# S4D convolution beside a sigmoid GLU on one core: GpSimd's share of the spectral products ahead of the weights, the first column half's last stage by quarters, another order of the frequency steps

## The chip, the cores and the metric

The kernel runs on one core of a Trainium2 chip. The metric is device time in microseconds (us) from the first to the last instruction of one launch. The engines carry the names that the profile gives them: PE (TensorE) with its weight loads PEld, DVE (VectorE), ACT (ScalarE), POOL (GpSimd), SP (SyncE, which here only issues DMAs).

## The reference, cut to what matters

```python
# L = 2048 tokens, D = 448 channels, N = 256 states, F = 1792
x  = A_u
xn = layernorm(x)
# part A: diagonal state space model as a long convolution
dt = exp(log_dt); A = -exp(log_A_real) + 1j * A_imag; C = (C_real + 1j * C_imag) * dt
K  = 2 * einsum("dn,dnl->dl", C, exp(A * dt * pos)).real          # one kernel of 2048 taps per channel
y  = irfft(rfft(xn, 4096) * rfft(K, 4096), 4096)[:2048] + xn * D_skip
# part B: GLU
h  = sigmoid(xn @ w_gate) * (xn @ w_up)
out = x + y + h @ w_down
```

## The kernel before, in words

Two generators, `conv()` and `glu()`, write the program. A loop at the bottom of the kernel calls whichever of them has the smaller `done[i] / total[i]`; each `yield` says how much work, in the planner's own units, was just written. `total` (L1141) holds the two sums. For `conv()` the last term is `17 * WS`, one `WS` for each frequency step of the last stage. So these two numbers decide how far the GLU has come when the convolution reaches a given point. Afterwards a list scheduler orders the instructions of each engine by its own estimate of times; `hp(HP)` around an instruction raises its priority there by 300. What an engine's queue then holds is run strictly in that order.

The GLU goes through fourteen tiles of 128 rows of F for the first 1024 tokens (half 0) and again for the second 1024 (half 1). For each tile and each block of 512 tokens, `gate` (L692) writes two groups of 11 matmuls (`gu`, L710): the gate half and the up half, each in three parts, because every float is split into a high and a low part (`wh`/`wl` for weights, `xh`/`xl` for tokens). ACT takes tanh of the gate group (`th`), DVE multiplies (`hf`, L721), ACT and DVE split the product (`hh` L726, `hl` L728). After a group of two or three tiles come the down matmuls (`po`, L824; 9 matmuls for each 128 tokens of a group of three) with DVE's addition into `acc` (L829). In half 1 five weight tiles are loaded and split by GpSimd itself: DMA of `wraw` from GpSimd's queue (L645, L647), `wh` (L772), `wl` (L773), DMA of `rdw` (L653), `dh` (L798), `dl` (L799). `wraw` and `rdw` share one buffer, so for one tile these steps follow each other. The others come back split from memory through SP's queue.

The convolution has three stages: constants; a generation stage `kgen` that builds the kernel's first transform (products `ko`, L619, from `Et` and `Ft` of DVE, L603 to L605); and `spectra`, the last stage. This has 17 steps of two kinds of columns: for each of two column halves h (224 channels each), eight groups of four frequencies named by k, in the order `ks`, and once k = 32 for both. One step is:

- `there` (L908): 32 small matmuls each into two PSUM tiles `pk` (the kernel's spectrum) and `px` (the input's). ACT copies one half of each (`oo`, L912); DVE forms sum and difference (`kk`, `xx`, L914 and L915). When these are done, `pk` and `px` are free again.
- the products: `yy` (L919) and `kk` (L920) on DVE, then two instructions on GpSimd, the differences of the one (L921) and the sums of the other (L922), then `sd` (L924, L925) on DVE. There is one buffer of `yy` and of `kk`.
- `back` (L937) of the step before, into the same `pk` and `px`; ACT copies them to `vt` (L943) and SP writes that to memory (`v_d`): one DMA for each half of the partitions (L957), but for k = 0 three (L953, L955).

When all eight groups of a column half are written, `vp` is read back (L963) and `last` (L973) makes the outputs of that half from it, in four quarters of four token blocks q = 0 to 3: 32 matmuls into `pk` for an even q, into `px` for an odd one, followed by DVE's additions (L982). For h = 0 the quarters come two at a time, behind two consecutive steps; for h = 1 all four come at the very end, between the GLU's last down matmuls. `out` hands the finished rows of the h = 0 half to SP, ACT and GpSimd in turn for writing.

On PE the program fixes the order of the two streams by hand: `sp_mm` and `glu_mm` hold the last matmul of the one and of the other, and every group is told to issue behind it.

Of the kernel before, what the change touches and what calls it, by code (L numbers as in the profile page):

```python
# [15 lines left out]
ALU = mybir.AluOpType  # L16
# [12 lines left out]
NFT = F // 128  # L29
WK = 5.5  # L30
WS = 7.0
HOLE = 6
AHEAD = 46
WP = 5
WX = 2
HELD = 9
LATE = 3.6
HP = 300
Y0 = (8, 1)
# [13 lines left out]
NCK = D // DC  # L53
# [74 lines left out]
def s4d_glu_kernel(ctx, tc, io):  # L128
    nc = tc.nc
    hp = tc.high_priority  # L130
# [107 lines left out]
    def out_end(src, b0, ds, engs=(nc.sync, nc.scalar)):  # L238
        for g in range(4):
            to = blocks(out_t, g, b0, src.shape[1])  # L240
            engs[g % len(engs)].dma_start(to[:, :, ds], src[32 * g : 32 * g + 32, :, ds])
# [606 lines left out]
    def spectra(pf):  # L848
# [16 lines left out]
        def work(n, sh, bufs):  # L865
            return spare[n].pop() if spare.get(n) else pf.tile(sh, F32, name=n, bufs=bufs)
# [22 lines left out]
        def after():  # L889
            return tc.issue_after(sp_mm[0].ins)  # L890

        def there(k, tb, sk, sx):

            n = 2 if k == 32 else 4
            np_ = 32 * n
            both = []
            for j, src in enumerate((sk, sx)):
                with after():
                    for c in range(2):
                        for g in range(n):  # L900
                            for p in range(2):
                                s = slice(64 * p, 64 * p + 64)
                                to = pb[j][32 * g : 32 * g + 32, p, H * c : H * c + H]
                                rhs = sx[s, g]
                                if src is sk:
                                    to, rhs = to.rearrange("p (g d) -> p g d", d=32), sk[s, :, g]
                                w = (t32[s, 0] if k == 32 else tb[s, g])[:, 32 * c : 32 * c + 32]
                                mm = nc.tensor.matmul(to, w, rhs, start=True, stop=True, skip_group_check=True)  # L908
                sp_mm[:] = [mm]
                ev, od = (half(pb[j][:np_, p, : 2 * H]) for p in range(2))  # L910
                oo = work("oo", [128, 2, H], 2)
                nc.scalar.copy(oo[:np_], od)  # L912
                t = work(("kk", "xx")[j], [128, 2, 2, H], 1)
                v.tensor_tensor(t[:np_, 0], ev, oo[:np_], ALU.add)  # L914
                v.tensor_tensor(t[:np_, 1], ev, oo[:np_], ALU.subtract)  # L915
                both.append(t[:np_])
            kk, xx = both
            yy = work("yy", [128, 2, 2, H], 1)[:np_]
            v.tensor_tensor(yy, kk, xx, ALU.mult)  # L919
            v.tensor_tensor(kk, kk, xx[:, :, ::-1], ALU.mult)  # L920
            nc.gpsimd.tensor_tensor(yy[:, :, 0], yy[:, :, 0], yy[:, :, 1], ALU.subtract)  # L921
            nc.gpsimd.tensor_tensor(yy[:, :, 1], kk[:, :, 0], kk[:, :, 1], ALU.add)  # L922
            sd = work("sd", [128, 2, 2, H], 2)
            v.tensor_tensor(sd[:np_, 0], yy[:, 0], yy[:, 1], ALU.add)  # L924
            v.tensor_tensor(sd[:np_, 1], yy[:, 0], yy[:, 1], ALU.subtract)  # L925
            return sd
# [32 lines left out]
        def turned(h, k, n=8):  # L959
            if h not in vp:  # L960
                vp[h] = pf.tile([128, 32, H], F32, name="vp", bufs=1)
            s = slice(k // 4, 128, n)
            nc.sync.dma_start(vp[h][s], v_d[h, s])  # L963

        def last(h, q):

            for p in range(2):
                s = slice(64 * p, 64 * p + 64)
                for i in range(2):
                    for g in range(4):  # L970
                        w = 16 * (q % 2) + 4 * g + 2 * (q // 2) + i
                        with after():
                            mm = nc.tensor.matmul(  # L973
                                pb[q % 2][32 * g : 32 * g + 32, p, H * i : H * i + H], wf[s, w], vp[h][s, w],
                                start=True, stop=True, skip_group_check=True,
                            )
            sp_mm[:] = [mm]
            ds = slice(H * h, H * h + H)
            acc = ac[:, 4 * q : 4 * q + 4] if q < 2 else accs[q]
            for p in range(2):  # L980
                a = acc[:, p::2, ds]
                v.tensor_tensor(a, a, half(pb[q % 2][:, p, : 2 * H]), ALU.add)  # L982
            if h == 1 and q < 3:
                out_end(acc, 4 * q, ds, *([[nc.gpsimd]] if q == 0 else []))
            elif h == 0 and q < 2:
                out(acc, 4 * q, h)
# [2 lines left out]
        lasts.append(last)  # L989
        nc.sync.dma_start(t32, io["c_t32"])  # L990
        nc.gpsimd.dma_start(bk, io["c_bk"])
        ks = [4, 20, 0, 16, 8, 24, 12, 28]
        steps = [(0, k) for k in ks] + [(1, k) for k in ks[-NTB:] + ks[:-NTB]]
        steps[1:1] = [(None, 32)]
        tabs = {}
        ld = [loads(*s) for s in steps[:NLD]]
        nc.gpsimd.dma_start(wf, io["c_wf"])
        prev, wait, due = None, [], []
        for n, (h, k) in enumerate(steps):

            sp_mm[:] = glu_mm
            cur = there(k, *ld[n])
            if (h, k) == (0, ks[-NTB - 1]):
                for k_ in ks[:-NTB]:
                    tabs.pop(k_)
            if n + NLD < len(steps):
                ld.append(loads(*steps[n + NLD]))
            glu_on[:] = [1]
            yield WS / 2
            sp_mm[:] = glu_mm  # L1010
            if prev is not None:
                back(*prev)
            if 4 <= n < 8:
                o = slice(2 * n - 8, 2 * n - 6)
                nc.sync.dma_start(ac[:, o], acc_d[:, o])
            if prev is not None and prev[1] < 32:
                wait.append(prev[:2])

            while len(wait) > 2 and not (due and wait[0][0] == 1):
                t, u = wait.pop(0), wait.pop(0)  # L1020
                turned(*t, 4)
                if u == (0, 28):
                    due = [n + 1]
            prev = (h, k, cur)
            if n == 11:
                total[1] -= LATE
            yield WS / 2
            if due and n >= due[0]:
                sp_mm[:] = glu_mm
                for q in (0, 1, 2, 3)[2 * (n - due[0]) : 2 * (n - due[0]) + 2]:  # L1030
                    last(0, q)
                if n == due[0] + 1:
                    due = []
        sp_mm[:] = glu_mm
# [95 lines left out]
    lasts, glu_mm, sp_mm, glu_on, outs, x1s, hfs, xls = [], [], [], [], [0], [0], [], []  # L1130
    xq, psc, raws, acl, marks, slots, pqs = list(x_first), [], [], [], [None, None], {}, []
    W1s, GGs, act = [], [], []
    gens = [conv(), glu()]
    total = [sum(Y0) + 11 * WP + 8 * WX + AHEAD + NCK * WK + HOLE + 17 * WS, 2 * (4 + NFT * 14.8) - HELD]
    done = [0.0, 0.0]
    done[0] += next(gens[0])
    held = False
# [38 lines left out]
```

## Time and profile before

| | us |
|---|---|
| three runs | 757.61, 762.92, 768.84 |
| median | 762.92 |
| the profiled execution's own time | 769.57 |
| its span, first to last instruction | 767.8 |
| busy: PE, DVE, POOL, ACT | 678.1, 602.3, 427.1, 423.1 |
| mean granted TensorE clock | 0.945 |

In a row of the timeline stand the start, the duration, the engine, the line, the operation, the output and the input, the number of instructions, and in brackets the idle time of the engine before it with what ended it. In the chain of waits stand start, duration and what ran. A row of the waits has the total, the number and the longest one. In a row of the windows come the stretch, its length, then the busy time of PE, PEld, DVE, ACT and POOL, the granted clock, the DMA engines' share and GB/s.

### The profile page before, as it was taken

Reading aid. Unit: us, or ns where it says so; the run is one execution under the profiler, and the core shown is the slowest. Engines: PE = TensorE matmul, PEld = TensorE weight load, DVE = VectorE, ACT = ScalarE, POOL = GpSimd, SP = SyncE. Lnnn points to the kernel's source line nnn. Section 1 sums busy time; section 2 is a strip of 40 time slices with the busy share of each in tenths; the row PEclk is TensorE's granted clock in tenths of the full one; section 3 lists DMA queues with packets and bytes.
Section 4 is the critical chain, followed back from the end, with each engine's and each line's share of the span. In section 5 each row is a group of like instructions: output and inputs, shape, how many; then the busy total and the mean of one; then the engine's idle time right before and its main releaser. Section 6 shows DMA issues by size and latency. Waiting matters only on the chain.

```text
span 767.8 us, 22542 instructions
## 1 busy us (share of the span) xinstructions
PE 678.1 (88%) x9477; PEld 520.6 (68%) x9477; DVE 602.3 (78%) x777; ACT 423.1 (55%) x651; POOL 427.1 (56%) x455
## 2 busy tenths in 40 slices
PE   3897699999998988888899999899899799968966
PEld 2664588877876877555778777788667567645754
DVE  6798996789998998876659988787397567777843
ACT  3544466477787888787377777767413222212310
POOL 2110065748889889974636776754146553675211
PEclk9997989999999999798999999999999999988997
DMA  9934265345234543344744134304588757775464
GB/s 209 208 126 160 79 200 178 117 137 177 78 102 151 180 118 96 116 151 144 229 136 146 38 95 141 93 20 142 149 260 233 213 159 205 214 206 163 114 161 126
DMA packets 93462, 114.58 MB, mean 149 GB/s; under 512 B 12848, under 2 KB 83056, under 8 KB 93104
## 3 DMA queue, kind: packets, MB, share of 16 engines
q1 hardware_dynamic: 71632, 92.54, 41.1%
q10 hardware_dynamic: 19248, 14.91, 6.9%
q0 software_dynamic: 2480, 5.67, 2.8%
q8 instruction: 75, 1.23, 0.7%
q14 instruction: 27, 0.22, 0.1%
HBM read 68.32 MB, written 44.76 MB: 147 GB/s over the span
## 4 chain that ended last, share of the span: by engine, by line
PE 34%; DVE 9%; issue 4%; POOL 4%; DMA 4%; ACT 2%; SPq 1%; ACTq 0%; DVEq 0%; POOLq 0%
PE gu L710 14%; PE po L824 7%; PE ko L619 4%; PE tr L535 2%; POOL yy L921 1%; DMA v_d<-vt 1%; POOL yy L922 1%; PE pk L908 1%; DVE yy L919 1%; DVE Ft L605 1%; DVE sd L925 1%; PE kp L561 1%; PE px L908 1%; DMA wraw<-in_B_w_up_dram 1%; DMA rdw<-in_B_w_down_dram 1%
## 5 line engine op out<-in xcount | busy, mean ns | idle before, releaser
L513 POOL TENSOR_TENSOR me<-me,pm 128x32 f32<-128x32 f32 (+1 forms) x168 | 147.5, 878 | 84.3 <-DVE Et L604 69.6
L513 POOL TENSOR_TENSOR mf<-mf,pm 128x64 f32<-128x64 f32 (+1 forms) x112 | 122.7, 1095 | 6.1
L710 PE MATMUL gu<-xh,wh 128*128 128x512 f32 x336 | 107.8, 431 | 6.4 <-DVE acc L829 4.8
L710 PE MATMUL gu<-xh,wl 128*128 128x512 f32 x336 | 99.5, 404 | 0.0
L710 PE MATMUL gu<-xl,wh 128*128 128x512 f32 x336 | 98.3, 397 | 0.5 <-DVE xl L218 0.5
L824 PE MATMUL po<-dh,hh 128*128 128x448 f32 (+1 forms) x227 | 87.1, 384 | 10.0 <-DVE hf L721 3.8
L605 DVE TENSOR_TENSOR Ft<-mf,S 128x1024 f32<-128x1024 f32 x56 | 80.5, 1437 | 13.5 <-PE ko L619 4.4
L604 DVE TENSOR_TENSOR Et<-me,S 128x1024 f32<-128x1024 f32 x56 | 79.1, 1412 | 14.2 <-ACT me L526 14.2
L710 PEld LDWEIGHTS gu<-xh,wh 128*128 128x128 f32 x336 | 64.6, 203 | 30.2 <-issue 10.0
L824 PE MATMUL po<-dl,hh 128*128 128x448 f32 (+1 forms) x227 | 84.1, 370 | 0.0
L603 DVE TENSOR_TENSOR Et<-me,S 128x1024 f32<-128x1024 f32 x56 | 77.3, 1384 | 8.2 <-ACT S L546 7.9
L824 PE MATMUL po<-dh,hl 128*128 128x448 f32 (+1 forms) x227 | 82.8, 368 | 0.0
L543 ACT ACTIVATE S<-tr 128x1024 f32<-128x1024 f32 x56 | 57.7, 1031 | 43.6 <-PE tr L535 28.8
L726 ACT CAST hh<-hf 128x512 fp32r<-128x512 f32 x56 | 34.9, 623 | 78.3 <-DVE hf L721 77.7
L619 PEld LDWEIGHTS ko<-Et,Ft 128*32 128x32 f32 x3584 | 56.1, 115 | 30.3 <-DVE Ft L605 13.6
L710 PEld LDWEIGHTS gu<-xh,wl 128*128 128x128 f32 x336 | 66.0, 197 | 15.1
L619 PE MATMUL ko<-Et,Ft 128*32 128x64 f32 x3584 | 65.9, 228 | 11.5 <-DVE Ft L605 11.5
L710 PEld LDWEIGHTS gu<-xl,wh 128*128 128x128 f32 x336 | 63.7, 191 | 16.0 <-issue 1.4
L546 ACT ACTIVATE S<-S,hpi 128x1024 f32<-128x1024 f32 x56 | 65.6, 1171 | 0.0
L721 DVE SCALAR_TENSOR_TENSOR hf<-th,gu 128x512 f32<-128x512 f32 x56 | 38.1, 680 | 32.8 <-PE gu L710 26.1
L829 DVE SCALAR_TENSOR_TENSOR acc<-po,acc 128x448 f32<-128x448 f32 (+1 forms) x81 | 48.2, 608 | 18.6 <-PE po L824 18.6
L728 DVE TENSOR_TENSOR hl<-hf,hh 128x512 fp32r<-128x512 f32 x56 | 51.4, 918 | 14.3 <-ACT hh L726 14.2
(212 smaller groups left out, 1357.9 us busy)
## 6 DMA issues: line engine op xcount, KB each, us to landing
sk_d<-sk ACTq DMA_DIRECT2D x14, 512.0 KB
sx<-x_d SPq DMA_DIRECT2D x64, 112.0 KB
skl<-sk_d SPq DMA_DIRECT2D x16, 448.0 KB
vp<-v_d SPq DMA_DIRECT2D x7, 896.0 KB
v_d<-vt SPq DMA_DIRECT2D x27, 224.0 KB
wt_d<-wh SPq DMA_DIRECT2D x9, 512.0 KB
wt_d<-wl SPq DMA_DIRECT2D x9, 512.0 KB
wl<-wt_d SPq DMA_DIRECT2D x9, 512.0 KB
```

What stands on the lines that cost most here:

```text
L513: ins = nc.gpsimd.tensor_tensor(m[:, :, w + a : 2 * w : n], m[:, :, a:w:n], par(base + i).unsqueeze(2).to_broadcast([128, 4 * DC, w // n]) ...
L543: nc.scalar.activation(rows(cs), pv, AF.Abs)
L546: sins[:] = [nc.scalar.activation(cs, cs, AF.Sin, scale=-TWO_PI, bias=hpi)]
L603: v.tensor_tensor(Et[:, :, :, 32:64], two(me[:, :, 32:64]), S[:, 1::-1], ALU.mult)
L604: v.tensor_tensor(Et[:, :, :, 0:32], two(me[:, :, 0:32]), S[:, 1:3, :, ::-1], ALU.mult)
L605: fts[:] = [v.tensor_tensor(Ft, two(mf), S[:, 3:5], ALU.mult)]
L619: nc.tensor.matmul(ko[32 * j : 32 * j + 32, sl], Ft[:, cc, DC * h + 4 * q + j], Et[:, cc, DC * h + 4 * q + j], start=(k == 0), stop=(k == ...
L710: glu_mm[:] = [nc.tensor.matmul(ps, a_, b_, start=(n == 0), stop=(n == len(mm) - 1))]
L721: marks[1] = v.scalar_tensor_tensor(hf, th, 1.0, pgu[1], ALU.add, ALU.mult)
L728: v.tensor_tensor(hl, hf, hh, ALU.subtract)
L824: glu_mm[:] = [nc.tensor.matmul(po[:, ds], a_[:, bs], w_[:, ds], start=(n == 0), stop=(n == 3 * fc - 1))]
L829: v.scalar_tensor_tensor(acc[:, b, ds], po[:, ds], 0.5, acc[:, b, ds], ALU.mult, ALU.add)
```

## The change

```diff
--- before.py
+++ after.py
@@ -914,12 +914,18 @@
                 v.tensor_tensor(t[:np_, 0], ev, oo[:np_], ALU.add)
                 v.tensor_tensor(t[:np_, 1], ev, oo[:np_], ALU.subtract)
                 both.append(t[:np_])
-            kk, xx = both
+            return both
+
+        def product(np_, kk, xx):
             yy = work("yy", [128, 2, 2, H], 1)[:np_]
             v.tensor_tensor(yy, kk, xx, ALU.mult)
             v.tensor_tensor(kk, kk, xx[:, :, ::-1], ALU.mult)
-            nc.gpsimd.tensor_tensor(yy[:, :, 0], yy[:, :, 0], yy[:, :, 1], ALU.subtract)
-            nc.gpsimd.tensor_tensor(yy[:, :, 1], kk[:, :, 0], kk[:, :, 1], ALU.add)
+            with hp(HP):
+                nc.gpsimd.tensor_tensor(yy[:, :, 0], yy[:, :, 0], yy[:, :, 1], ALU.subtract)
+                nc.gpsimd.tensor_tensor(yy[:, :, 1], kk[:, :, 0], kk[:, :, 1], ALU.add)
+            return yy
+
+        def halves(np_, yy):
             sd = work("sd", [128, 2, 2, H], 2)
             v.tensor_tensor(sd[:np_, 0], yy[:, 0], yy[:, 1], ALU.add)
             v.tensor_tensor(sd[:np_, 1], yy[:, 0], yy[:, 1], ALU.subtract)
@@ -989,7 +995,7 @@
-        ks = [4, 20, 0, 16, 8, 24, 12, 28]
+        ks = [4, 20, 8, 24, 0, 16, 12, 28]
         steps = [(0, k) for k in ks] + [(1, k) for k in ks[-NTB:] + ks[:-NTB]]
@@ -999,7 +1005,9 @@
             sp_mm[:] = glu_mm
-            cur = there(k, *ld[n])
+            np_ = 64 if k == 32 else 128
+            kk, xx = there(k, *ld[n])
+            cur = halves(np_, product(np_, kk, xx))
@@ -1028,7 +1036,9 @@
             if due and n >= due[0]:
                 sp_mm[:] = glu_mm
                 for q in (0, 1, 2, 3)[2 * (n - due[0]) : 2 * (n - due[0]) + 2]:
+                    sp_mm[:] = glu_mm
                     last(0, q)
+                    yield WS / 2
                 if n == due[0] + 1:
                     due = []
@@ -1131,7 +1141,7 @@
-    total = [sum(Y0) + 11 * WP + 8 * WX + AHEAD + NCK * WK + HOLE + 17 * WS, 2 * (4 + NFT * 14.8) - HELD]
+    total = [sum(Y0) + 11 * WP + 8 * WX + AHEAD + NCK * WK + HOLE + 19 * WS, 2 * (4 + NFT * 14.8) - HELD]
```

Splitting `there` into three functions writes the same instructions in the same sequence. The two GpSimd instructions get the raised priority. The quarters of h = 0 are separated by `yield`s, so that the GLU's matmuls are written between them. The second column half now ends with k = 8 and 24 where it ended with 0 and 16. The convolution's total is two steps larger.

The change moves instructions at many places, because the planner's total and the scheduler's order hang together. Three of them follow; line numbers from L915 on differ between the two programs, since the new one is longer (L921 and L922 become L924 and L925, L937 becomes L943, L963 becomes L969, L973 becomes L979).

PE at the first two quarters of h = 0. First before: `back` of a step, both quarters, `there` of the next step, then a GLU group.

```order
L937 MATMUL pk_7100<-sd_8308,bk_7098 64x224 x8
L937 MATMUL px_7101<-sd_8308,bk_7098 64x224 x8
L973 MATMUL pk_7100<-vp_7102,wf_7097 32x224 x16
L973 MATMUL px_7101<-vp_7102,wf_7097 32x224 x16
L908 MATMUL pk_7100<-skl_8201,tb_7751 32x224 x16
L908 MATMUL px_7101<-sx_8200,tb_7751 32x224 x16
L710 MATMUL gu_8586<-xh_4131,wh_8320 128x512 x3
```

And now:

```order
L943 MATMUL px_7053<-sd_8253,bk_7050 64x224 x8
L979 MATMUL pk_7052<-vp_7054,wf_7049 32x224 x16
L824 MATMUL po_8437<-dh_7492,hh_7606 128x448
L824 MATMUL po_8437<-dl_7493,hh_7606 128x448
L824 MATMUL po_8437<-dh_7492,hl_7607 128x448
L824 MATMUL po_8437<-dh_7734,hh_7852 128x448
L824 MATMUL po_8437<-dl_7735,hh_7852 128x448
L824 MATMUL po_8437<-dh_7734,hl_7853 128x448
L824 MATMUL po_8437<-dh_7978,hh_8091 128x448
L824 MATMUL po_8437<-dl_7979,hh_8091 128x448
L824 MATMUL po_8437<-dh_7978,hl_8092 128x448
L979 MATMUL px_7053<-vp_7054,wf_7049 32x224 x16
```

The nine down matmuls, the last of their tile group, now stand between the quarters, and a `gu` group of 11 (not shown) between the second quarter and `there`. The second pair of quarters has a `gu` group ahead of, between and behind its two.

POOL at the last two weight tiles. Before, from the out writes of the first quarters on:

```order
L236 DMA out_0_dram<-ac_7093 32x4x224 x2
L921 TENSOR_TENSOR yy_8569<-yy_8569 128x2x224
L772 CAST wh_8898<-wraw_8899 128x1024
L922 TENSOR_TENSOR yy_8569<-kk_8545 128x2x224
L773 TENSOR_TENSOR wl_8906<-wraw_8899,wh_8898 128x1024
L653 DMA rdw_8993<-in_B_w_down_dram 128x448
L798 CAST dh_8991<-rdw_8993 128x448
L799 TENSOR_TENSOR dl_8992<-rdw_8993,dh_8991 128x448
L921 TENSOR_TENSOR yy_8728<-yy_8728 128x2x224
L922 TENSOR_TENSOR yy_8728<-kk_8704 128x2x224
```

And now, from the end of the last tile but one:

```order
L925 TENSOR_TENSOR yy_8535<-kk_8511 128x2x224
L653 DMA rdw_8771<-in_B_w_down_dram 128x448
L798 CAST dh_8769<-rdw_8771 128x448
L799 TENSOR_TENSOR dl_8770<-rdw_8771,dh_8769 128x448
L645 DMA wraw_8903<-in_B_w_gate_dram 128x3x128
L647 DMA wraw_8903<-in_B_w_gate_dram 64x128 x2
L645 DMA wraw_8903<-in_B_w_up_dram 128x3x128
L647 DMA wraw_8903<-in_B_w_up_dram 64x128 x2
L772 CAST wh_8902<-wraw_8903 128x1024
L773 TENSOR_TENSOR wl_8910<-wraw_8903,wh_8902 128x1024
L924 TENSOR_TENSOR yy_8732<-yy_8732 128x2x224
L653 DMA rdw_8997<-in_B_w_down_dram 128x448
```

Before, one step's pair stands between the last tile's DMAs and its `wh`. Now the tile's whole chain of two transfers and four instructions stands between the pair of step 13 (`yy_8535`) and that of step 14 (`yy_8732`); steps are counted from 1 here.

SP behind the last step's `back`. Before:

```order
L953 DMA v_d_64<-vt_9100 32x224 x2
L955 DMA v_d_64<-vt_9100 32x3x224 x4
L963 DMA vp_8792<-v_d_64 16x7168
L957 DMA v_d_64<-vt_9137 32x8x224
L963 DMA vp_8792<-v_d_64 16x7168
```

And now:

```order
L969 DMA vp_8796<-v_d_64 32x7168
L963 DMA v_d_64<-vt_9104 32x8x224 x2
L969 DMA vp_8796<-v_d_64 16x7168
L963 DMA v_d_64<-vt_9137 32x8x224
L969 DMA vp_8796<-v_d_64 16x7168
```

The six writes of k = 0 have become two of k = 8, and the rest is as it was. The six of the second column half now belong to its first step, the tenth of seventeen, and there stand ahead of the loads (`skl`, `sx`, `tb`) for the third step after.

## The prediction

> **What bounds the kernel now.** I read the busy time by stage first, then PE's waits in the last stage, then the chain of waits through it, then single rows. The windows, one for the generation stage and two for the last stage up to its last `back`:
>
> ```profile
> 180.00:557.00 377.00, 349.77 (x6277) 275.79 (x6275) 308.76 (x321) 279.14 (x407) 266.99 (x282) 0.95 0.41 125
> 557.00:678.00 121.00, 109.70 (x1411) 79.18 (x1409) 90.42 (x125) 31.48 (x60) 67.60 (x58) 0.96 0.76 215
> 678.00:737.00 59.00, 48.16 (x688) 33.22 (x684) 45.13 (x61) 15.17 (x29) 27.37 (x27) 0.88 0.54 153
> ```
>
> PE is busy 93% of the generation stage, 91% and 82% of the last stage's two parts. The generation stage is thus mostly bound by PE; from 557 to 737 PE stands still for 22 us. Its waits from 557 us on:
>
> ```profile
> PE pk L937 <- DVE kk L915: 9.9, 6, 3.0
> PE pk L973 <- DMA vp<-v_d: 5.7, 1, 5.7
> PE pk L908 <- DVE ac L982: 5.2, 1, 5.2
> PE pk L908 <- DVE acc L982: 3.3, 1, 3.3
> ```
>
> The first row is `back`, which may not write into `pk` before the next step's `kk` has been read out of it; `kk` stands behind `sd` in DVE's queue, and `sd` waits for GpSimd. The third and fourth are the two pairs of quarters. A wait costs more than its length: after the first pair, `there` and a group of 11 take 1.75 + 1.49 + 3.14 us, where an undisturbed step takes 0.92 + 0.76 + 2.72, because the granted clock is low there (0.88 in that window).
>
> ```profile
> 575.88 0.92 PE pk L908 x32
> 576.80 0.76 PE px L908 x32
> 577.56 2.72 PE gu L710 x11
> 580.27 0.92 PE pk L937 x16
> 683.33 1.75 PE pk L908 x32
> 685.08 1.49 PE px L908 x32
> 686.57 3.14 PE gu L710 x11
> 701.94 3.94 PE gu L710 x11
> ```
>
> **The sum, part by part.** It is made against the profiled execution's own 769.57 us, which lies 6.65 above the median of the runs; at the end I take the difference off the median.
>
> *Pacing.* With two more `WS` in the convolution's total the GLU falls behind. Counted in the two orders, 275 `gu` matmuls follow the last `ko` before, 308 now: three groups of 11, 3 x 2.72 = 8.2 us of PE, leave the generation stage and join the last one. There they cost 8.2. In the generation stage they bring 8.2 if PE is all that binds it, and nothing if DVE is (a rival below). At 93% busy it is near the first: -7.0 there, +8.2 here.
>
> *First pair of quarters.* DVE's additions of one quarter:
>
> ```profile
> 682.21 1.08 DVE ac L982 x2
> ```
>
> PE's wait of 5.24 and the slow stretch behind it (6.38 - 4.40 = 1.98) cost 7.2. Now nine `po` lie between the two quarters and a group of 11, 2.72 us, between the second and `there`, so that the additions, 1.08 a quarter, have time; and no weight stands in GpSimd's queue at this place to make `sd` late, which stands ahead of them in DVE's. -7.2 (least -4, if DVE's wait for `sd` remains in part).
>
> *GpSimd's priority.* The chain runs through GpSimd's weights from 595.87 to 620.88:
>
> ```profile
> 595.87 0.58 POOL L653 DMA_DIRECT2D rdw<-in_B_w_down_dram  x1
> 601.51 1.27 POOL L798 CAST dh<-rdw 128x448 fp32r<-128x448 f32 x1 [5.06 <-DMA rdw<-in_B_w_down_dram]
> 602.86 1.86 POOL L799 TENSOR_TENSOR dl<-rdw,dh 128x448 fp32r<-128x448 f32 x1
> 605.02 0.78 POOL L645 DMA_DIRECT2D wraw<-in_B_w_gate_dram  x1 [0.30 <-POOL dl L799]
> 607.61 1.04 POOL L647 DMA_DIRECT2D wraw<-in_B_w_up_dram  x2
> 608.67 1.17 POOL L921 TENSOR_TENSOR yy<-yy 128x448 f32<-128x448 f32 x1
> 614.17 1.04 POOL L772 CAST wh<-wraw 128x1024 fp32r<-128x1024 f32 x1 [3.11 <-DMA wraw<-in_B_w_up_dram]
> 615.29 3.08 POOL L773 TENSOR_TENSOR wl<-wraw,wh 128x1024 fp32r<-128x1024 f32 x1
> 616.19 3.14 DVE L920 TENSOR_TENSOR kk<-kk,xx 128x896 f32<-128x896 f32 x1
> 618.34 2.00 POOL L921 TENSOR_TENSOR yy<-yy 128x448 f32<-128x448 f32 x1
> ```
>
> The `yy` at 608.67 stood behind a transfer and the instructions shown. PE's waits here, and the next `yy` in the chain:
>
> ```profile
> 600.32 0.99 PE L937 MATMUL pk<-sd,bk 32*64 32x224 f32 x16 [1.26 <-DVE kk L915]
> 614.07 0.99 PE L937 MATMUL pk<-sd,bk 32*64 32x224 f32 x16 [3.03 <-DVE kk L915]
> 626.42 0.99 PE L937 MATMUL pk<-sd,bk 32*64 32x224 f32 x16 [1.61 <-DVE kk L915]
> ```
>
> ```profile
> 628.61 2.01 POOL yy L921
> ```
>
> The waits are 5.9 us of the 9.9. The new order has whole pairs of `yy` ahead of `wh` at these steps. The other three waits of the row stay, since there no weight stood in the way: from 618.34 to 628.61 DVE and GpSimd needed 10.3 us for their own round, where PE needs 8.2 for a step with two groups (2 x 2.72, 1.68, 1.05). Bounds: 0, and the whole row of 9.9. I take -5.0, most of the three waits.
>
> Beside this stands the Trainium skill, SBUF — State Buffer, section Who interferes with whom: a DVE instruction with two SBUF inputs and a GpSimd instruction that reads SBUF exclude each other for the whole instruction. The trace agrees: `kk` took 3.14 us beside `wl`, and the mean of `wl` is 2.67. By that rule priority only chooses who waits, and this term would be 0; it is a rival below.
>
> *The new wait.* In GpSimd's queue the whole chain of the last weight tile now stands ahead of step 14's `yy`. I count from the end of the last `po` before the second quarter, which frees a `dh` buffer. PE would reach step 14's `back` after eight groups (21.8), three `there` (5.0), two `back` (2.1) and three quarters (3.0): 31.9. GpSimd first makes the last tile but one: `dh` to `wl` took 16.9 in the rows above (601.51 to 618.37), and its `yy` pair adds 2.3 (twice the 1.17 of 608.67). Then the last tile: 22.5 by the rows above (595.87 to 618.37). Quicker ones are
>
> ```profile
> 675.40 0.58 POOL L653 DMA_DIRECT2D rdw<-in_B_w_down_dram  x1 [0.30 <-POOL wl L773]
> 678.46 0.56 POOL L798 CAST dh<-rdw 128x448 fp32r<-128x448 f32 x1 [0.20 <-DMA rdw<-in_B_w_down_dram]
> 680.07 1.13 POOL L799 TENSOR_TENSOR dl<-rdw,dh 128x448 fp32r<-128x448 f32 x1
> 694.21 2.35 POOL L773 TENSOR_TENSOR wl<-wraw,wh 128x1024 fp32r<-128x1024 f32 x1
> ```
>
> by which `dh` to `wl` takes 14.7, and a whole tile 0.58 + 2.5 (landing) + 0.6 + 1.1 + 0.3 + 3.7 (issue of `wraw`) + 5.5 (landing, 608.65 to 614.17) + 1.1 + 2.4 = 17.7. I take the middle of each: 15.8 and 20.1. Behind the last `wl` follow `yy`, a DMA issue and `yy` again (2.9), then `sd` and `kk`, four additions like those of a quarter (2.2): 15.8 + 2.3 + 20.1 + 5.1 = 43.3. PE then waits 43.3 - 31.9 = 11.4 in all, plus about 2 of slow clock, as behind the first pair of quarters. That takes the place of the second pair's wait (3.28, and 1.75 + 1.49 + 3.94 - 4.40 = 2.78 behind it, 6.1 before), which would otherwise vanish: -6.1 + 13.4 = +7.3. Bounds: -6.1 if `yy` is not held up; with the slow rows throughout 46.8 - 31.9 = 14.9, 2.8 of slow clock and again -6.1, so +11.6. Behind this `yy` in GpSimd's queue stand the last `rdw` and its `dh`, which no one needs before the last `po`; behind `sd` in DVE's queue stands `kk`, and that is what PE waits for.
>
> *Step order.* The tail before, and ahead of it an earlier write of the same kind:
>
> ```profile
> 677.39 2.86 DMA v_d<-vt
> ...
> 739.29 5.86 DMA v_d<-vt
> 745.21 5.01 DMA vp<-v_d
> ```
>
> ```profile
> 738.39 0.68 ACTq L957 DMA_DIRECT2D v_d<-vt  x1
> 738.71 0.53 SPq L963 DMA_DIRECT2D vp<-v_d  x1
> ```
>
> SP's half of the last write is issued 0.9 behind ACT's (739.29 against 738.39), since `vp` of k = 0 waits ahead of it. With two writes instead of six it can go at 738.39: -0.9 at least. If it also lands in 2.86 instead of 5.86, the gain is 3.9. PE waits 5.7 there, so it counts in full. I take -1.5. The six writes, now at step 10, delay the loads behind them by some 3 us; these are issued three steps (25 us) ahead, which hides it. Without that cover it would be 3.
>
> Sum: -7.0 + 8.2 - 7.2 - 5.0 + 7.3 - 1.5 = -5.2. On its own basis 764.4; on the median 757.7 us.
>
> **The rivals.** *The new wait doesn't come* (chance 0.28): transfers land sooner, or PE is late anyway, and the second pair's wait goes as well. The term is -6.1 instead of +7.3: 744.3 us, faster by 2.4%. For it: three of the terms in 43.3 are landings, and a landing of `rdw` was anything from 2.5 to 5.1 us. Against it: even the quicker rows throughout (14.7 + 2.3 + 17.7 + 5.1 = 39.8) end 7.9 us behind PE.
>
> *The generation stage gives nothing back* (0.17). Of PE's waits from 180 to 557 us the longest row is
>
> ```profile
> PE ko L619 <- DVE Ft L605: 11.5, 9, 2.8
> ```
>
> With less GLU in between, these waits could grow by as much as leaves. Place: that stage, where DVE is busy 82%. Price: 7.0, so 764.7, slower than before by 1.8. It decides when the stage shrinks by less than 1.8. Against it: PE is the busier one there.
>
> *Priority buys nothing* (0.13): each weight instruction still holds up one of DVE's two-input instructions, as `wl` did `kk` at 616.19. The term is 0: 762.7, no change. For it: that row. Against it: what held `yy` at 608.67 was a landing transfer, in which GpSimd did nothing.
>
> **How the numbers follow.** The forecast has 0.42: 757.7 us, within 2% of 762.92 (747.7 to 778.2), which is about what a measurement of this kernel can tell from no change. With two of its terms at their bounds it runs from about 748 to 767. Three quarters of the first rival and a tenth of the forecast make faster 0.25; slower by over 2% needs the new wait at its upper bound and another term lost, 0.08; 0.67 is left for the same. The range holds the first rival's value and, above, the second with the new wait at its bound: 742 to 772, wider than the forecast's own bounds by what the rivals need.
>
> **What would show it.** Right: the last `ko` some 7 us earlier; `there` right behind the first two quarters without a wait; GpSimd idle ahead of the last `wh`, with DVE's `sd` of step 14 waiting for it and PE for `kk`, 8 us or more; the final `vp` issued 1 us or more earlier after the last `back`. Wrong: the generation stage as long as before; no wait of PE over 4 us between the quarters and the tail, which would be the first rival; the waits of `back` still 9 us or more in total before the quarters.

## The result, and the profile after

| | before | after |
|---|---|---|
| median (us) | 762.8, 20 runs (756.32 to 771.21) | 765.36, 20 runs (761.96 to 771.75) |
| ratio | | 1.0051, 95% interval 1.0028 to 1.0075 |
| the profiled execution's own time | 769.57 | 767.31 |
| its span | 767.8 | 765.5 |

The change is slower by half a per cent, a small loss that the interval still separates from nothing, where 757.7 us and a gain of 5.2 were forecast. The ratio is taken from the fast runs alone; the medians of all runs lie 2.6 us, or 0.34%, apart. The two profiled executions differ from the medians: that of before lies 6.8 above its own, that of after 1.95 above its own, so side by side they show a gain of 2.3 that is not there. What each place costs is therefore read inside a stage, and the size of an effect from the medians.

The windows of the changed kernel, for the same stretches as before (columns as there; the stages now start at other times):

```profile
180.00:557.00 377.00, 350.11 (x6395) 275.29 (x6384) 322.69 (x328) 280.19 (x411) 273.50 (x283) 0.97 0.42 127
557.00:678.00 121.00, 109.01 (x1372) 78.89 (x1371) 89.56 (x124) 29.11 (x57) 60.62 (x52) 0.93 0.73 202
678.00:737.00 59.00, 50.27 (x613) 34.66 (x611) 42.84 (x57) 15.31 (x30) 31.34 (x32) 0.94 0.53 150
```

The second row has fallen from a clock of 0.96 to 0.93 and PE is still busy for only 109 of 121 us, and the third has risen from 0.88 to 0.94. What was mended at the quarters has come back earlier in the stage. PE's waits from 540 us on say the same:

```profile
PE pk L943 <- DVE kk L915: 6.1, 5, 3.6
PE pk L943 <- issue: 4.7, 1, 4.7
PE px L908 <- DVE acc L988: 3.0, 1, 3.0
PE pk L943 <- DVE sd L930: 2.6, 1, 2.6
PE pk L979 <- DMA out_dram<-acc: 2.0, 1, 2.0
...
PE pk L908 <- DVE acc L988: 1.5, 1, 1.5
PE gu L710 <- POOL wl L773: 1.2, 1, 1.2
```

`vp` and the first pair of quarters are gone from the list (5.7 and 5.2 before). In their place stand 4.7 and 3.6 us ahead of `back` (L943). Both are at the same kind of place, the first step of the stage and the fifth. Here is the first, from the timeline of GpSimd, DVE and PE:

```profile
555.70 1.14 POOL L925 TENSOR_TENSOR yy<-kk 128x448 f32<-128x448 f32 x1
556.79 1.04 POOL L772 CAST wh<-wraw 128x1024 fp32r<-128x1024 f32 x1
556.88 1.43 DVE L930 TENSOR_TENSOR sd<-yy 128x448 f32<-128x448 f32 x1 [1.07 <-POOL yy L925]
557.91 2.60 POOL L773 TENSOR_TENSOR wl<-wraw,wh 128x1024 fp32r<-128x1024 f32 x1
558.23 2.76 DVE L931 TENSOR_TENSOR sd<-yy 128x448 f32<-128x448 f32 x1
...
562.75 1.39 PE L943 MATMUL pk<-sd,bk 32*64 32x224 f32 x12 [4.66 <-issue]
```

The pair of `yy` is ready early and no weight holds it up. But the weight tile that stood ahead of it now starts in the same microsecond as DVE's `sd`, which reads what `yy` has written. The first `sd` takes 1.43 us, the second 2.76, about as long as `wl` beside it, 2.60. Together they are 2.95 us longer than two undisturbed ones. Where no weight runs an `sd` takes 0.62; beside the smaller `dh` and `dl` it takes 0.95 and 1.56. Before, there was one `sd` of 2.76 in the stage, at 694.28 between the quarters. Now there are two, and both early. At 598.83 the same thing happens again:

```profile
599.95 2.66 POOL L773 TENSOR_TENSOR wl<-wraw,wh 128x1024 fp32r<-128x1024 f32 x1
600.27 2.82 DVE L931 TENSOR_TENSOR sd<-yy 128x448 f32<-128x448 f32 x1
606.27 1.17 PE L943 MATMUL pk<-sd,bk 32*64 32x224 f32 x16 [3.60 <-DVE kk L915]
```

So the weights were moved off one link of the chain and onto the next, and there they cost more. At the end of the program, the new wait that the forecast had put on step 14's `back` is found earlier, at the second pair of quarters:

```profile
690.77 1.15 POOL L925 TENSOR_TENSOR yy<-kk 128x448 f32<-128x448 f32 x1
691.95 0.62 DVE L930 TENSOR_TENSOR sd<-yy 128x448 f32<-128x448 f32 x1 [8.52 <-POOL yy L925]
694.23 0.99 PE L908 MATMUL pk<-skl,tb 64*32 64x224 f32 x32 [1.48 <-DVE acc L988]
698.18 1.85 PE L908 MATMUL px<-sx,tb 64*32 64x224 f32 x32 [2.96 <-DVE acc L988]
704.09 2.38 POOL L773 TENSOR_TENSOR wl<-wraw,wh 128x1024 fp32r<-128x1024 f32 x1
706.44 2.00 POOL L924 TENSOR_TENSOR yy<-yy 128x448 f32<-128x448 f32 x1
```

DVE stands idle for 8.52 us for the `yy` of step 13 (behind the landing of `wraw`, `wh` and `wl` of the last tile but one), and the additions of the quarters stand behind that `sd`. PE waits for them twice, 1.48 and 2.96 us, ahead of the two halves of `there`. The additions of the second of these quarters stand behind one more DVE instruction that runs beside a weight. It is `hl`, which takes 0.69 us where no weight runs beside it (604.37):

```profile
695.39 1.12 POOL L799 TENSOR_TENSOR dl<-rdw,dh 128x448 fp32r<-128x448 f32 x1
695.46 1.60 DVE L728 TENSOR_TENSOR hl<-hf,hh 128x512 fp32r<-128x512 f32 x1 [0.69 <-ACT hh L726]
```

### The profile page after: what moved, and what is told of

Read it like the earlier page. It is cut to its first block, busy times and chain, and to the rows that moved or that the text cites. A ratio compares the mean times of both kernels' runs of the same rounds, so it can differ in the third digit from the quotient of the medians.

```text
span 765.5 us, 22546 instructions
## 1 busy us (share of the span) xinstructions
PE 680.3 (89%) x9477; PEld 522.3 (68%) x9477; DVE 612.8 (80%) x777; ACT 421.1 (55%) x651; POOL 427.8 (56%) x455
## 3 DMA queue, kind: packets, MB, share of 16 engines
HBM read 68.32 MB, written 44.76 MB: 148 GB/s over the span
## 4 chain that ended last, share of the span: by engine, by line
PE 50%; DVE 23%; issue 7%; POOL 7%; DMA 7%; ACT 5%; SPq 1%; DVEq 0%; ACTq 0%; POOLq 0%
PE gu L710 22%; PE po L824 11%; PE ko L619 7%; PE tr L535 3%; POOL yy L925 2%; POOL yy L924 2%; DVE yy L921 2%; DVE acc L829 2%; DVE Ft L605 2%; DMA wraw<-in_B_w_up_dram 1%; DVE sd L931 1%; DVE hf L721 1%; DVE Et L604 1%; PE kp L561 1%; DVE hl L728 1%
## 5 line engine op out<-in xcount | busy, mean ns | idle before, releaser
L513 POOL TENSOR_TENSOR me<-me,pm 128x32 f32<-128x32 f32 (+1 forms) x168 | 151.4, 901 | 72.4 <-DVE Et L604 57.8
L513 POOL TENSOR_TENSOR mf<-mf,pm 128x64 f32<-128x64 f32 (+1 forms) x112 | 124.7, 1114 | 6.0
L710 PE MATMUL gu<-xh,wh 128*128 128x512 f32 x336 | 105.6, 423 | 8.4 <-DVE acc L829 4.8
L824 PE MATMUL po<-dh,hh 128*128 128x448 f32 (+1 forms) x227 | 89.7, 395 | 5.7 <-DVE hf L721 2.7
L603 DVE TENSOR_TENSOR Et<-me,S 128x1024 f32<-128x1024 f32 x56 | 80.7, 1444 | 11.5 <-ACT S L546 11.5
L604 DVE TENSOR_TENSOR Et<-me,S 128x1024 f32<-128x1024 f32 x56 | 78.8, 1407 | 10.8 <-ACT me L526 7.0
L824 PE MATMUL po<-dl,hh 128*128 128x448 f32 (+1 forms) x227 | 86.1, 379 | 0.0
L710 PEld LDWEIGHTS gu<-xh,wh 128*128 128x128 f32 x336 | 62.3, 197 | 33.2 <-issue 9.7
L824 PE MATMUL po<-dh,hl 128*128 128x448 f32 (+1 forms) x227 | 84.7, 377 | 0.0
L924 POOL TENSOR_TENSOR yy<-yy 128x448 f32<-128x448 f32 (+1 forms) x17 | 30.0, 1765 | 73.5 <-DVE yy L921 73.5
```

The lines of the kernel that those rows point to most:

```text
L513: ins = nc.gpsimd.tensor_tensor(m[:, :, w + a : 2 * w : n], m[:, :, a:w:n], par(base + i).unsqueeze(2).to_broadcast([128, 4 * DC, w // n]) ...
L603: v.tensor_tensor(Et[:, :, :, 32:64], two(me[:, :, 32:64]), S[:, 1::-1], ALU.mult)
L604: v.tensor_tensor(Et[:, :, :, 0:32], two(me[:, :, 0:32]), S[:, 1:3, :, ::-1], ALU.mult)
L710: glu_mm[:] = [nc.tensor.matmul(ps, a_, b_, start=(n == 0), stop=(n == len(mm) - 1))]
L824: glu_mm[:] = [nc.tensor.matmul(po[:, ds], a_[:, bs], w_[:, ds], start=(n == 0), stop=(n == 3 * fc - 1))]
```

## The experiments

Theory A, formed from these rows: the larger total alone changes GpSimd's order, so that weights run beside `sd`, and that is the loss; the quarters and the step order gain what their waits were worth. The rivals: the larger total loses by itself, with or without weights (B); the quarters only move their wait (C); at a larger total still, the generation stage gives nothing back (D).

One part needed no run. The raised priority of GpSimd's two instructions changes no instruction's place: the changed kernel without it has the same order on all five engines as with it, and the kernel before has the same order when it is added. So the change consists of three effective parts: S, the step order; T, the total of 19 steps; Q, the quarters with `yield`s. The order of GpSimd that the forecast credited to the priority comes from T, and at the last two weight tiles from T and Q together.

T and Q also belong together in the planner's count. A step yields `WS / 2` twice, so 17 steps make the 17 `WS` of the old total. Q's four new `yield`s of `WS / 2` add two `WS` to what is counted as done, and T adds two to the total. In the planner's units (`WS` is 7), the convolution ends with 559 done of 559 before, 573 of 559 with Q alone, 559 of 573 with T alone, and 573 of 573 with both. So with Q alone the planner takes it for finished two steps early and writes the GLU too soon. With T alone it never takes it for finished, and the GLU comes late: three groups of 11 and nine more `po` then stand behind the last `back`. Beside Q, 18 steps are one too few by this count and 21 two too many.

### S, T, Q alone, and Q with S

Each is an edit of the kernel before. S:

```diff
-        ks = [4, 20, 0, 16, 8, 24, 12, 28]
+        ks = [4, 20, 8, 24, 0, 16, 12, 28]
```

> The kernel before with the new step order alone (ks with 8, 24 ahead of 0, 16). Theory A (the tail gains by the step order, what was lost is lost between the last ko and the last back): the tail from the last back to the end takes 26 to 28 us instead of the 30.5 of before, the rest as before; 757 to 761 us against 762.8, ratio about 0.996. Rival: the shorter tail of the changed kernel comes from elsewhere (the GLU's lag): 762.8, ratio within 0.999 to 1.001.

T:

```diff
-    total = [sum(Y0) + 11 * WP + 8 * WX + AHEAD + NCK * WK + HOLE + 17 * WS, 2 * (4 + NFT * 14.8) - HELD]
+    total = [sum(Y0) + 11 * WP + 8 * WX + AHEAD + NCK * WK + HOLE + 19 * WS, 2 * (4 + NFT * 14.8) - HELD]
```

> The kernel before with 19 WS instead of 17 in the convolution's total and nothing else. Theory A (the two more WS put three GLU groups into the last stage and let GpSimd's wh and wl start right behind yy, where sd needs the same port): the last ko some 8 to 10 us earlier, back of the second step waits 4 to 5 us and another back 3 to 4, with sd taking 2.8 instead of 0.6 us there; 765 to 771 us, ratio 1.003 to 1.010. Rival (the pacing is neutral, 8.2 us leave one stage and join the other): 760 to 764, ratio 0.998 to 1.002.

Q; with S's line beside it, Q + S:

```diff
                 for q in (0, 1, 2, 3)[2 * (n - due[0]) : 2 * (n - due[0]) + 2]:
+                    sp_mm[:] = glu_mm
                     last(0, q)
+                    yield WS / 2
```

Q alone: 

> The kernel before with the quarters of h = 0 one by one and the GLU between them, total and step order as before. Theory A (quarters between GLU groups take away PE's two waits and the slow clock behind them, 7.2 and some 3 to 6 us): 751 to 756 us, ratio 0.985 to 0.991. Rival (the waits move behind the weights, since GpSimd's queue holds wh, wl and dl of two tiles around these quarters): 760 to 765, ratio 0.997 to 1.003.

Q + S: 

> Quarters one by one and the new step order, the total as before: the change without its 19 WS. Theory A: the sum of the two parts, 748 to 754 us, ratio 0.981 to 0.988, so some 10 us under the changed kernel. Rival (without the larger total the GLU runs out of work in the last steps, and PE waits there instead): 760 to 766 us, with PE waits of over 5 us between the last quarter of h = 0 and the last back.

Here and below, each ratio is to runs of the kernel before that were made beside those of the row:

| | median (us) | ratio to before, 95% interval |
|---|---|---|
| S | 762.35 | 0.9981 (0.9942 to 1.0019) |
| T | 768.51 | 1.0037 (0.9998 to 1.0075) |
| Q | 761.97 | 0.9972 (0.9939 to 1.0005) |
| Q + S | 764.59 | 0.9993 (0.9948 to 1.0038) |

T is the only part that loses, about as much as the whole, though its interval just reaches 1. Its trace shows the collision, at the first and the fifth step of its stage:

```profile
553.72 2.59 POOL L773 TENSOR_TENSOR wl<-wraw,wh 128x1024 fp32r<-128x1024 f32 x1
554.03 2.76 DVE L925 TENSOR_TENSOR sd<-yy 128x448 f32<-128x448 f32 x1
558.55 1.40 PE L937 MATMUL pk<-sd,bk 32*64 32x224 f32 x12 [4.66 <-issue]
...
601.64 1.61 PE L937 MATMUL pk<-sd,bk 32*64 32x224 f32 x16 [3.58 <-DVE kk L915]
```

It is not all that T costs. A wait of 5.5 us stands behind the last tile but one, at 700.69, and the groups left over lengthen the end: from the last `back` to PE's last matmul 27.1 us instead of 25.0. These runs do not tell how much of T's loss each of them is.

Q should have been worth 1 to 1.5% and is at most 0.6%, so that part of theory A falls. Where its gain went stands in its own timeline. At the first quarters PE waits 1.99 us instead of 5.24, and no longer at the second pair; but the last two steps have little left between their parts:

```profile
675.28 1.43 PE L908 MATMUL px<-sx,tb 64*32 64x224 f32 x32 [1.99 <-DVE ac L982]
...
712.06 0.99 PE L937 MATMUL pk<-sd,bk 32*64 32x224 f32 x16 [2.60 <-DVE kk L915]
714.56 1.75 PE L908 MATMUL pk<-skl,tb 64*32 64x224 f32 x32
719.84 1.40 PE L937 MATMUL pk<-sd,bk 32*64 32x224 f32 x16 [2.44 <-DVE kk L915]
726.01 1.09 PE L937 MATMUL pk<-sd,bk 32*64 32x224 f32 x5 [3.33 <-DVE sd L924]
```

Between the `there` at 707.71 and the `back` at 712.06 stands no GLU group any more, nor between the next two, since the groups have been used up between the quarters. These three waits are 8.4 us, where the profile of before has one of 2.32 in this place; the first half of `there` at 714.56 takes 1.75 instead of 0.99 behind the first of them. The GLU's matmuls are a fixed stock, and a gap covered at one place opens at another. Q + S, for which 748 to 754 us was expected, came as its rival said: the same three steps wait 2.64, 3.99 and 3.3 us there.

S moved the end as far as forecast or further in its profile: from the last `back` to PE's last matmul 21.0 us instead of 25.0. The median shows at most 0.6% of it. Q without S has a tail of 20.3 us. What both have lost is the late issue of the last `v_d` write, here in S, on both queues at once:

```profile
735.27 0.60 SPq L957 DMA_DIRECT2D v_d<-vt  x1
735.27 0.68 ACTq L957 DMA_DIRECT2D v_d<-vt  x1
```

In Q the six writes of k = 0 are still there, but PE's late last steps leave SP time: it issues that `vp` at 727.48 and the last write, with ACT's, at 729.31. So S is one way to this gain, and not the only one.

### Q with T, and the whole with 18 steps

Q + T is the kernel before with the lines of Q and T above. It is the changed kernel with the old step order, and without the raised priority, which moves nothing.

> The changed kernel with the old order of the frequency steps: quarters with GLU between them, and 19 steps in the total. Theory A: the loss of the larger total (1.004 alone) and the small gain of the quarters (0.997 alone) add: 1.000 to 1.005, two sd of 2.8 us, waits of 4 to 5 and 3 to 4 us ahead of back in the first steps of the last stage. Rival C (the quarters gain only where the total makes room for GLU between them, and the other order of the steps is what loses): under 0.997.

The other is the changed kernel with a total of 18 steps:

```diff
-    total = [sum(Y0) + 11 * WP + 8 * WX + AHEAD + NCK * WK + HOLE + 19 * WS, 2 * (4 + NFT * 14.8) - HELD]
+    total = [sum(Y0) + 11 * WP + 8 * WX + AHEAD + NCK * WK + HOLE + 18 * WS, 2 * (4 + NFT * 14.8) - HELD]
```

> The changed kernel with 18 steps in the convolution's total instead of 19. In GpSimd's order the first weight tile of the last stage stands between the two yy of a step, as in the kernel before, and the next two stand behind whole pairs. Theory A: the size of the loss goes with the number of sd that run beside wl: one or two sd of over 2 us instead of two, waits of back over 3 us once or not at all, 760 to 765, ratio to before 0.997 to 1.003. Rival B (the total itself costs): half of the loss, ratio 1.001 to 1.004, whatever sd takes.

| | median (us) | ratio to before, 95% interval |
|---|---|---|
| Q + T | 767.47 | 1.0045 (1.0015 to 1.0076) |
| the change with 18 steps | 764.7 | 1.0037 (1.0007 to 1.0067) |

With T, Q brings nothing measurable (1.0045 against 1.0037 for T alone), and the old step order is no better than the new one. The run with 18 steps tells A and B apart badly. It has three `sd` of 2.8 us (at 553.94, 672.31 and 691.63), but no wait ahead of `back` behind `kk` above 2.7. Its longest are 4.9 us for additions of a quarter ahead of `there` and 4.1 ahead of the last `back`, which has no GLU in front of it. Its 1.0037 lies within B's range of 1.001 to 1.004 and above A's, which ended at 1.003; its interval reaches into both, and its median into A's 760 to 765 us.

### No weights on GpSimd in the last stage

This takes the suspected cost away. The five tiles come back split from memory through SP's queue, as the other nine do. It costs more traffic (HBM reads 72.09 MB instead of 68.32, writes 52.30 instead of 44.76), and GpSimd then has little but the `yy` pairs and the output writes in this stage. It takes away more than the collision: the `yy` that stand behind a `wl` or a transfer go with it. So the times show what the weights cost as a whole, and the rows show where.

```diff
-RAW = set(GROUPS[0] + GROUPS[1][1:])
+RAW = set()
```

In the changed kernel: 

> The changed kernel, but GpSimd splits no weights in the last stage: the five tiles that it split come back split from memory through SP's queue, like the others (four stores and four loads more per tile pair, no raw loads). Theory A (with 19 steps in the total, weights start right behind yy and run against DVE's sd, so that sd takes 2.8 us instead of 0.6 and PE waits 4.7 and 3.6 us ahead of back): every sd takes 0.6 us, no wait of back behind kk is over 3 us, the waits of back in the last stage fall from 14 us to under 9; beside the kernel before without splitting it is no longer slower: ratio of the two medians 0.985 to 1.000. Rival B (the larger total itself costs: less GLU ahead of the last stage only moves PE's work, and the round of DVE and GpSimd through products and sums, some 10 us a step, sets the pace with or without weights): sd takes 0.6 us, but the waits of back stay 10 us or more, and the ratio of the two stays 1.003 or above.

In the kernel before: 

> The kernel before, with the same edit: GpSimd splits no weights in the last stage. It is the base for the changed kernel with that edit. Theory A: every sd takes 0.6 us, and the three waits of back in the stretch of the second and third weight tile (1.3, 3.0 and 1.6 us in the profile of before) shrink to under 1 us each; the two waits behind pairs of quarters (5.2 and 3.3) stay at 2 to 4, since the additions still follow at once. 752 to 764 us. Rival B: the waits of back stay near 10 us and the time within 0.3% of the kernel before.

With T alone: 

> The kernel before without splitting on GpSimd in the last stage, plus the total of 19 steps alone. Base: the same without the larger total, 755.32 us, 0.988 of the kernel before. Theory A (what the larger total lost was weights against sd): with no weights there the larger total loses nothing: 750 to 756 us, ratio to the kernel before 0.981 to 0.989. Rival B (the larger total loses by itself): it adds its 0.4% here too: 758 us or more, ratio 0.991 or above.

With Q and S: 

> The kernel before without splitting on GpSimd in the last stage, plus the quarters with GLU between them and the other order of the steps, the total left at 17. Theory A: with no weights late behind them the quarters keep their gain of 4 to 5 us, which stood in the profile as 3.7 + 0.7 us of waits and slow clock behind: 749 to 753 us, ratio 0.980 to 0.987. Rival C (the gain of the changed kernel without splitting comes from the larger total, the quarters' waits only move): 755 us or more, ratio 0.987 or above.

With the whole change and 21 steps: 

> The changed kernel without splitting on GpSimd, with 21 steps in the total instead of 19. Theory A: still more GLU beside the last stage covers the round of DVE and GpSimd in more steps, and the waits of back (7.7 us with 19) shrink further: 746 to 750 us, ratio 0.976 to 0.982, unless the GLU's rest then outlasts the convolution at the end. Rival D (the gain is spent at 19, what GLU is moved only moves PE's work and the tail grows by its down matmuls): 750 to 756, ratio 0.982 to 0.990.

The kernel before had a median of 763.49 us beside the first and the fourth row and of 765.19 beside the others, so rows are compared by their ratios:

| no weights on GpSimd, and | median (us) | ratio to before, 95% interval | with them on GpSimd |
|---|---|---|---|
| nothing else | 755.32 | 0.9877 (0.9837 to 0.9918) | 1 |
| T | 752.68 | 0.9848 (0.9797 to 0.9898) | 1.0037 |
| Q + S | 759.39 | 0.9944 (0.9908 to 0.9979) | 0.9993 |
| the whole change | 749.89 | 0.9806 (0.9754 to 0.9858) | 1.0051 |
| the whole change, 21 steps | 754.51 | 0.9887 (0.983 to 0.9943) | |

B's forecast is not met: without the weights T no longer loses, and the 0.991 or more that B asked for lies outside its interval. The whole change, a loss of 0.5% with weights on GpSimd, then gives the lowest time of all, 0.7% below its own base (0.9806 / 0.9877 = 0.9928; 0.986 to 0.999, with the widths of the two intervals combined). That comparison has a flaw, a new wait in the base, which follows below. At the place of the first collision the same instructions now read, in the changed kernel without splitting:

```profile
557.77 1.14 POOL L925 TENSOR_TENSOR yy<-kk 128x448 f32<-128x448 f32 x1
558.94 0.62 DVE L930 TENSOR_TENSOR sd<-yy 128x448 f32<-128x448 f32 x1 [1.07 <-POOL yy L925]
559.48 0.62 DVE L931 TENSOR_TENSOR sd<-yy 128x448 f32<-128x448 f32 x1
```

Every other `sd` of that trace takes 0.6 us too, and of PE's waits from 535 us on these are the longest:

```profile
PE pk L943 <- DVE kk L915: 3.7, 6, 1.0
PE pk L943 <- DVE sd L930: 2.4, 1, 2.4
PE pk L943 <- issue: 1.7, 1, 1.7
```

The two waits that the collision was held to blame for stand in the same trace, and the order of PE is the same in both kernels:

```profile
561.86 0.98 PE L943 MATMUL pk<-sd,bk 32*64 32x224 f32 x16 [1.71 <-issue]
601.57 0.99 PE L943 MATMUL pk<-sd,bk 32*64 32x224 f32 x16 [0.56 <-DVE kk L915]
```

They were 4.66 and 3.60 and are now shorter by 2.95 and 3.04 us. The two pairs of `sd` have become shorter by as much: 1.43 + 2.76 - 2 x 0.62 = 2.95, and 1.43 + 2.82 - 2 x 0.62 = 3.01. So at these places it is `sd` beside `wh` and `wl` that PE waited for, and the rest of the first wait was there without it.

The quarters have no wait of their own left. Those of the kernel before with the same edit are these:

```profile
PE pk L908 <- DMA skl<-sk_d: 6.9, 1, 6.9
PE pk L908 <- DVE ac L982: 3.7, 1, 3.7
PE pk L973 <- DMA out_dram<-acc: 3.4, 1, 3.4
PE pk L937 <- DVE kk L915: 3.2, 5, 1.3
PE pk L937 <- DVE sd L924: 2.3, 1, 2.3
```

The waits of `back` behind `kk` are down from 9.9 us to 3.2 here as well, so weights on GpSimd cost the kernel before about 1.2%, net of what the edit brings in. The 6.9 us for `skl`, a load ahead of the stage's first step, is such a cost. It is there in both kernels without weights that have 17 steps (6.7 us in Q + S) and not in the two with 19. Its cause is open. It limits what the table says of T: a loss of T by itself, and the 0.7% (5.4 us) of the whole change, are no larger than this one wait of the base. So it stays open whether T costs anything by itself. That the collision cost what it did at its two places does not depend on it.

Q + S without T was the surprise: expected at 749 to 753, it came at 759.39, above its base, though the two intervals still touch. The quarters themselves behave as forecast, with one wait left:

```profile
682.34 0.99 PE L908 MATMUL px<-sx,tb 64*32 64x224 f32 x32 [0.45 <-DVE ac L982]
...
718.18 1.40 PE L937 MATMUL pk<-sd,bk 32*64 32x224 f32 x12 [2.64 <-DVE kk L915]
725.96 0.98 PE L937 MATMUL pk<-sd,bk 32*64 32x224 f32 x16 [1.79 <-DVE kk L915]
732.12 1.08 PE L937 MATMUL pk<-sd,bk 32*64 32x224 f32 x5 [4.11 <-DVE sd L924]
```

The last three rows are those of Q alone again: 8.5 us at the last steps, which have no GLU left. The base, with the same wait for `skl`, has one of 2.3 there, so the missing groups are what Q + S lost against it. With T, three more groups lie behind the generation stage, and only the 2.4 above remains: T supplies the cover that the quarters use up. C holds in this form.

With 21 steps the time is that of D, though the interval still touches that of 19. The waits in the generation stage grow (`ko` behind `Ft` 15.8 us instead of 12.1 with 19, `kp` 7.1 instead of 4.7 between 180 and 535 us), and the last stage starts no sooner, at 552.8 instead of 550.1. Most of the loss is at the end: three groups of 11 and nine `po` more than with 19 stand behind the last `back`, as in T alone, and from there to the end of the span it takes 33.0 us instead of 25.4.

## Why the prediction was wrong

*Pacing: right in size.* Last generation matmul 541.2 instead of 551.9 us, first `there` 548.0 instead of 557.2: -9.2 for -7.0. The other profiles with weights on GpSimd bear it out: with 17 steps the first `there` starts at 551.5 to 558.1 (four profiles, mean 555.0), with 19 at 543.8 to 548.0 (three, mean 545.5). The 8.2 us of GLU came back in the last stage as said. What the forecast did not see is the term's other worth: those three groups are the cover that Q needs at the last steps.

*First pair of quarters: right.* No wait at all behind it, -7.2. `there` now follows an undisturbed group:

```profile
671.44 1.01 PE L979 MATMUL px<-vp,wf 64*32 64x224 f32 x32
...
675.10 0.99 PE L908 MATMUL pk<-skl,tb 64*32 64x224 f32 x32
```

*GpSimd's priority: the step that failed.* The forecast said that whole pairs of `yy` now stand ahead of `wh`, and took -5.0 of the three waits there, with bounds of 0 and -9.9. The first half is true, though the order came from the pacing and not from the priority. But the reasoning stopped at `yy`. It did not ask where the weights go that no longer stand in front. They go right behind, into the time of `sd`, the next link of the same chain, where they lengthen two instructions from 0.62 to 1.43 and 2.76 us. From the first `there` to the last `back` PE took 190.8 us instead of 180.1. Of these 10.7 us, +8.2 is GLU and -7.2 the first pair, so this term and the next come to +9.7, where the forecast had +2.3. To part the two, I compare the stretch from the first `there` to the `back` that follows the `there` of step 13. It took 132.44 us before (557.20 to 689.64) and 131.58 now (548.02 to 679.60). PE does the same work in both, but for twelve `po` more now, some 2.6 us. Without these it is 3.5 us shorter now, where the first pair alone took 7.2 off: this term is about +3.7, not -5.0. It lies outside the bounds that were given, which excluded a loss. Of the waits alone little is left over (11.6 us now, 10.7 before without the first pair's); most of the +3.7 is slower matmuls, above all behind the two long ones, and the granted clock of the stretch from 557 to 678 fell from 0.96 to 0.93. The forecast had named waits of 9 us or more before the quarters as a sign of being wrong, and this sign came.

The material for it stood in the text. The rival "priority buys nothing" (0.13) rested on a `kk` of 3.14 us beside `wl`, and `sd` is another DVE instruction with two inputs in SBUF. Even that rival put the cost at 0 and not above. By the rule of the Trainium skill cited there, SBUF — State Buffer, section Who interferes with whom, an `sd` that meets `wl` waits until `wl` is done, and the trace agrees (2.76 beside 2.60, 2.82 beside 2.66, 0.62 without). What the rule leaves to the reader is which of DVE's instructions it hits, and that decides the price. Held up by the weights, `yy` had cost three waits of 1.3, 3.0 and 1.6 us, 5.9 in all. They are gone, but `sd` beside `wh` and `wl` put 2.95 and 3.0 us into two others, which are now 4.7 and 3.6.

*The new wait: right in size, wrong in place.* GpSimd's chain was counted at 43.3 us from the end of the last `po` before the second quarter. It ended at 712.5, 41.0 us behind that `po`. PE did not meet it at step 14 (0.41 us there), because it had already lost its time at the second pair, to the last tile but one: 1.18 us for `wl`, 1.48 and 2.96 for the additions, and slow clock behind. What is left of the 9.7, +6.0, is this term, for +7.3. That the size came near is in part luck, since the time was lost at another place than the one it was counted for.

*Step order: right in direction.* The last `v_d` write goes out on both queues at 739.85, and the tail from the last `back` on is 3.7 us shorter in the profiles (26.7 instead of 30.5) instead of 1.5. The single runs show that the late steps of Q would have brought it as well, and that S alone measures as no change.

Summed up on the two profiles: -9.2 + 8.2 - 7.2 + 3.7 + 6.0 - 3.7 = -2.2, which is their difference to rounding. The forecast was -5.2, and on the medians the change lost 2.6. The 4.9 us between are the distances of the two profiled executions from their medians (6.8 and 1.95). The forecast took the 6.65 of before off its result as if it would stay the same after the change; in which stage it lay is not known.

## What to carry to other kernels

When an instruction is moved out of the way of a chain, look at what it runs beside in its new place, on every other engine, before booking the gain: here the weights cost PE some 3.7 us more beside `sd` than ahead of `yy`, and of what was tried only taking them off the engine paid (2.4% of the changed kernel). Filler work of one stream is a stock: list every gap that it covers now before spending it on another. Whoever adds `yield`s to a planned stream must raise its total by as much, and test the two as one change. And a setting that is tuned beside a hidden cost (17 or 19 steps) must be tried again once that cost is gone, since its sign may turn: the whole change went from a loss of 0.5% to a gain of 0.7%, of which the base's wait for `skl` may be a part.

## What the hardware showed that was not expected

Two short `sd` of 0.62 us became 1.43 and 2.76 beside one `wh` and `wl`, so that the first, which meets `wh` of 1.04, also pays, and a 2.66-us instruction that nothing waited for at that moment was followed by a wait of PE of 3.6 us. Waits of 1 to 3 us close together were followed by a lower clock: `there`'s second half took 1.85 us at 698.18, behind waits of 1.18, 1.48 and 2.96 within 9 us, at a granted clock of 0.50 from 698 to 700 us, where it takes 0.96 undisturbed. A single wait of 2.32 us at the last `back` of the kernel before, at 735.87, was not: its matmuls took 0.35 to 0.42 us each, no longer than others there.
